# Another hand-written order for the first slots of a sparse-attention and FFN kernel

## The chip, the core and the metric

One Trainium2 chip, one of its cores. A core has a matrix engine (TensorE; PE in the profile, its weight loads PEld), a vector engine (VectorE, DVE), a scalar engine (ScalarE, ACT), GpSimd (POOL) and a queue engine for transfers (SyncE, SP), each with its own stream of instructions in a fixed order, and DMA engines that serve all queues. The metric is the device time of one execution in microseconds (us); lower is better. A time is the median of three runs; the profile is of one further execution.

## The reference

Attention with two sparse masks over 8 batches x 8 heads, 576 tokens, 64 wide, and then, for all 4608 tokens of width 512, a feed-forward network that multiplies two projections and has no nonlinear function:

```python
scores = scale * np.matmul(q, k.transpose(0, 1, 3, 2))
rel = pos[:, None] - pos[None, :]
mask_local = (rel >= 0) & (rel < 32)
mask_strided = (rel >= 0) & (pos[None, :] % 32 == pos[:, None] % 32)
masks = [mask_local if h < H // 2 else mask_strided for h in range(H)]
attn = softmax(np.where(masks, scores, -1e9)) @ v
x = attn.transpose(0, 2, 1, 3).reshape(4608, 512)
out = ((x @ w1) * (x @ w2)) @ w3 @ w_out        # w1, w2: 512x1024; w3: 1024x1024; w_out: 1024x512
```

## The kernel before, in words

**Pairs.** Two heads of a batch make a pair; there are 32, four to a batch. In each batch pairs 0 and 1 (of four) have the local mask, 2 and 3 the strided one. A pair i goes through these steps, each a small function of the code:

- `load_qk` (L88): q and k are loaded by GpSimd's queue with a cast to f16, into one of four tiles `s16` that q and k of a pair share. A local pair takes one DMA each for q and k (L100), a strided one two each, one a head (L105).
- `load_v` (L108): v of a local pair comes by SP's queue in f32 into `vsL`, three DMAs (L117, L119); `gate` puts a small memset on DVE ahead of it (L115). v of a strided pair comes by GpSimd's queue, four DMAs (L130).
- `emit_T` (L292): PE transposes q and k (L301) into two banks of the pool `psA`; copies bring them back, q's of a local pair on ACT or, where `cp` is given, on DVE (L309), q's of a strided pair on DVE (L314), k's on ACT (L309, L315).
- `emit_S` (L318): PE makes the scores in two banks of the pool `psF` (L333, L339), DVE adds the mask (L345).
- `emit_max` (L348), `emit_sub` (L356) on DVE, `emit_exp` (L364) on ACT.
- `emit_norm` (L375): DVE sums and inverts (L380, L382), then a product on GpSimd or, with `dve`, on DVE (L383).
- `emit_cast_v` (L277) and `shift_v` (L284), for local pairs: v's cast to f16 on GpSimd, ACT or DVE (L281), and a second copy of it, shifted by 32 rows, by two DMAs of SP.
- `emit_P` (L389): PE transposes the probabilities into a `psA` bank (L401) and ACT or DVE copies them out (L404). From pair 9 on a DMA does this.
- `emit_V` (L407): probabilities times v on PE in two `psF` banks (L421, L438), copied into `xT` by ACT and DVE (L426, L442 to L446).

`psA` has two banks and `psF` six; everything that PE writes draws on them.

**Weights.** w3 and w_out are multiplied once, into `wfh`. `load_w3(c)` (L210) loads two of the eight row groups of w3, a quarter of it, `load_wo(c)` (L207) a half of w_out, and `load_w` (L203) a half of w1 or w2. `fold_t(mc)` (L218) transposes a row group with eight matmuls (L223) and copies it (`w3T`, L225) on DVE or ACT; `fold_m(mc, half)` (L228) multiplies it by half of w_out, four matmuls (L233), and after the second half casts the result (L236).

**Masks.** `make_maskL` (L144) makes the local mask with four instructions on GpSimd and copies on ACT. `make_sel` (L159) makes a small pattern on GpSimd; `make_maskS` (L165) copies it twice on DVE (L168), multiplies it on PE (`mps`, L170), turns it into the mask on DVE (L172) and finishes it on GpSimd (L176).

**FFN.** Tokens go in nine chunks of 512. A chunk has eight a-pieces (x times w1, L248, copied by ACT, L252), eight b-pieces (x times w2, L258, multiplied on DVE, L261) and four out-pieces (times `wfh`, L269, copied by ACT, L274, stored by SP). `feed(us, batches)` (L475) puts pieces into the order until a credit in us is used up: 0.87 for an a- or b-piece, 1.74 for an out-piece. The first four a- and b-pieces of a chunk use the first halves of w1 and w2, the others the second halves.

**The order.** `manual_schedule` (L503) takes the instructions of each engine in the order in which these functions are called. Up to L674 this order is a list written out by hand: pairs 0 to 8, the folding of the weights and the first chunk. From L675 on (`for n in range(9, NP + 2)`) a loop gives the order for pairs 9 to 31. So each engine's queue is fixed, and an instruction that waits holds up all that stands behind it on its engine; for GpSimd, which issues most loads, that includes the loads.

Of the kernel before, what the change touches and what calls it, by code (L numbers as in the profile page):

```python
# [27 lines left out]
def kernel(  # L28
# [130 lines left out]
    def make_sel():  # L159
        nc.gpsimd.memset(sel, 1.0)  # L160
        for sg in (1, -1):
            nc.gpsimd.affine_select(out=sel, in_=sel, compare_op=ALU.is_ge, fill=0.0, base=0,
                                    pattern=[[0, 22], [sg, 3]], channel_multiplier=-sg)
# [327 lines left out]
    def zero_S():  # L491
        for t in qTS + prS:
            nc.vector.memset(t, 0.0)

    def zero_L(i):
        nc.vector.memset(kTL[i][:, 0:QB], 0.0)
        nc.vector.memset(vsL[i][HALF:P, LC - 1], 0.0)
        nc.vector.memset(vhL[i][0:QB, 0, 0], 0.0)
        nc.vector.memset(prL[i][:, LB, :], 0.0)
# [1 line left out]
    dve = nc.vector  # L501
    cp, act, pool = nc.vector.tensor_copy, nc.scalar.copy, nc.gpsimd.tensor_copy
    with tc.manual_schedule():  # L503
        zero_S()
        load_v(1)
        load_qk(0, "k")
        make_maskL()
        load_qk(1, "k")
        make_identity(nc, id16)
        load_qk(0, "q")  # L510
        load_qk(1, "q")
        load_v(0, True)
        load_w3(2, 2)
        load_qk(2, "k")
        load_qk(2, "q")
        make_sel()
        load_wo(0)
        load_qk(3, "k")
        zero_L(1)
        zero_L(0)  # L520
        emit_T(0, cp)
        load_w3(0, 2)
        emit_S(0)
        emit_T(1)
        load_qk(3, "q")
        emit_max(0)
        emit_cast_v(1, cp)
        nc.vector.memset(wz, 0.0)
        load_wo(4)
        make_maskS()  # L530
        load_v(3)
        emit_sub(0)
        emit_exp(0)
        emit_norm(0)
        emit_S(1)
        emit_T(2)
        fold_t(3, act)
        fold_t(2, act)
        emit_cast_v(0, cp)
        emit_max(1)  # L540
        load_w3(4, 2)
        emit_sub(1)
        load_qk(4, "k")
        emit_exp(1)
        fold_m(3, 0)
        load_qk(4, "q")
        fold_m(2, 0)
        emit_S(2)
        emit_norm(1)
        shift_v(0)  # L550
        emit_T(3)
        load_w(w1r, w1h, 0)
        load_v(2)
        fold_t(0, cp)
        fold_t(1, act)
        emit_P(0)
        emit_S(3)
        emit_max(3)
        load_w(w2r, w2h, 0)
        load_qk(5, "q")  # L560
        emit_max(2)
        fold_m(1, 0)
        shift_v(1)
        fold_m(1, 1, cp)
        fold_m(2, 1)
        load_qk(5, "k")
        emit_sub(3)
        fold_m(3, 1, cp)
        emit_sub(2)
        emit_exp(3)  # L570
        emit_norm(3)
        emit_P(1)
        fold_m(0, 0)
        emit_exp(2)
        fold_m(0, 1)
        fold_t(4, cp)
        fold_t(5, cp)
        emit_V(0)
        load_qk(6, "q")
        load_qk(6, "k")  # L580
        emit_V(1)
        emit_norm(2, dve)
        emit_T(4)
        fold_m(5, 0)
        load_w3(6, 2)
        fold_m(5, 1)
        emit_P(3)
        emit_P(2, cp)
        fold_m(4, 0)
        emit_V(2)  # L590
        emit_V(3)
        emit_S(4)
        load_qk(7, "k")
        feed(3.04, 1)
        emit_max(4)
        load_qk(7, "q")
        emit_sub(4)
        emit_T(5, cp)
        feed(2.61, 1)
        load_w(w1r, w1h, 1)  # L600
        emit_S(5)
        emit_T(6)
        emit_max(5)
        load_w(w2r, w2h, 1)
        emit_exp(4)
        fold_m(4, 1, cp)
        fold_t(6, act)
        fold_t(7, act)
        emit_sub(5)
        load_v(4, True)  # L610
        load_qk(8, "k")
        emit_T(7)
        emit_S(6)
        emit_max(6)
        fold_m(6, 0)
        fold_m(7, 0)
        emit_sub(6)
        emit_exp(6)
        emit_norm(4)
        load_qk(8, "q")  # L620
        emit_exp(5)
        load_v(5, True)
        emit_S(7)
        feed(1.46, 1)
        fold_m(6, 1)
        load_qk(9, "q")
        emit_norm(6, dve)
        emit_max(7)
        load_qk(9, "k")
        load_qk(10, "q")  # L630
        emit_cast_v(5, act)
        emit_norm(5)
        feed(0.43, 1)
        fold_m(7, 1, cp)
        emit_P(4, cp)
        emit_cast_v(4, act)
        feed(1.03, 1)
        load_v(6)
        shift_v(5)
        shift_v(4)  # L640
        load_qk(10, "k")
        load_v(8)
        load_v(10)
        feed(2.77, 1)
        emit_T(8)
        load_v(7)
        load_v(9, True)
        emit_sub(7)
        feed(2.17, 1)
        emit_P(6)  # L650
        emit_S(8)
        emit_exp(7)
        emit_norm(7, dve)
        emit_P(5, cp)
        emit_max(8)
        feed(2.17, 1)
        emit_sub(8)
        emit_T(9, cp)
        emit_V(4, cp)
        load_qk(13, "q")  # L660
        emit_V(5, cp)
        emit_exp(8)
        load_qk(12, "q")
        load_qk(11, "k")
        emit_V(6)
        emit_P(7)
        emit_cast_v(8, act)
        shift_v(8)
        load_qk(11, "q")
        emit_cast_v(9, cp)  # L670
        emit_norm(8)
        load_qk(13, "k")
        load_qk(12, "k")
        feed(3.17, 1)  # L674
        for n in range(9, NP + 2):  # L675
            full = (n - 1) // 4
            first = full - 1 if n % 4 == 1 else full
            f = 5.2
            if n < NP:
                shift_v(n)  # L680
                emit_S(n)
            if n + 1 < NP:
                emit_T(n + 1)
            if n + 5 < NP:
                load_qk(n + 5)
            for i in (n + 3, n + 2):
                if i < NP and where(i)[2] == (i == n + 3):
                    load_v(i)
            for i in (n - 3, n - 2):
                if i + (3 if by_dma(i) and i % 4 < 3 else 2) == n:  # L690
                    emit_V(i)
            if n < NP:
                emit_max(n)
            feed(0.1 * f, first)
            if n < NP:
                emit_sub(n)
                emit_exp(n)
                emit_norm(n)
                if n + 1 < NP:
                    emit_cast_v(n + 1)  # L700
            feed(0.15 * f, first)
            if n <= NP and not by_dma(n - 1):
                emit_P(n - 1)
            feed(0.55 * f, full)
            if n < NP and n % 2 == 1:
                for i in (n - 1, n):
                    if by_dma(i):
                        emit_P(i)
            feed(0.2 * f, full)
        feed(1e9, B)  # L710
# [31 lines left out]
```

## Time and profile before

| | us |
|---|---|
| median of three runs (lowest, highest) | 271.19 (270.99, 271.27) |
| the profiled execution | 270.49 |
| its span, first to last instruction | 268.7 |
| PE busy / DVE / POOL / ACT | 250.3 / 178.4 / 152.7 / 139.1 |
| PE's first transpose starts | 9.33 |
| PE's first fold_m starts | 18.00 |
| PE's first a-piece starts | 36.52 |
| PE reaches emit_S(9), the loop's first step | 67.68 |
| mean DMA rate over the span | 144 GB/s |

The profiled execution's own time is 1.8 us above its span. The page gives for each engine a busy share, then rows of 40 equal slices (6.7 us each) in tenths, then the chain of work that ended last, the costliest groups of instructions and the transfers. A "wait" names the engine and line that stood idle and what released it.

### The profile page before, as it was taken

To read this page: it belongs to the slowest core of one execution; us is meant where nothing else is said; L and a number is where in the kernel's file an instruction comes from. 1 tells how busy PE (TensorE), PEld (TensorE's weight loads), DVE (VectorE), ACT (ScalarE), POOL (GpSimd) and SP (SyncE) were. 2 spreads that over 40 slices of the span, in tenths; PEclk is the share of its full clock that TensorE was granted. 3 is DMA by queue.
4 is the path that set the end of the run, shared out by engine and by line. 5 is a ranking of instruction groups with operands and counts; after the bars stand their busy time and mean duration, and the time that the engine had idled before them with its cause. 6 is when DMAs were issued, how large, how long until landed. Compare 5 with 4: busy or idle time off the path is not lost.

```text
span 268.7 us, 9825 instructions
## 1 busy us (share of the span) xinstructions
PE 250.3 (93%) x4186; PEld 130.3 (48%) x4186; DVE 178.4 (66%) x357; ACT 139.1 (52%) x253; POOL 152.7 (57%) x236
## 2 busy tenths in 40 slices
PE   0288999999999999999999999999999999999995
PEld 0255656455554555554555455544554444444443
DVE  3378849999778768868886787678768823432210
ACT  3254756576655664666566466546655444333322
POOL 7688673498984896489468856886683110000000
PEclk9999999999999999999999999999999999999999
DMA  6999999999999699998998998996575152002113
GB/s 123 175 209 222 194 189 164 174 162 227 190 195 169 111 225 199 113 188 185 125 155 219 194 146 77 253 177 107 82 181 102 29 111 78 2 1 78 39 60 139
DMA packets 66237, 38.75 MB, mean 144 GB/s; under 512 B 45588, under 2 KB 60944, under 8 KB 66192
## 3 DMA queue, kind: packets, MB, share of 16 engines
q0 software_dynamic: 22112, 17.29, 43.3%
q1 hardware_dynamic: 44080, 20.82, 38.5%
q8 instruction: 33, 0.54, 0.8%
q14 instruction: 12, 0.10, 0.1%
HBM read 39.24 MB, written 9.44 MB: 181 GB/s over the span
## 4 chain that ended last, share of the span: by engine, by line
PE 75%; DMA 9%; DVE 8%; POOL 3%; issue 2%; ACT 2%; POOLq 0%; DVEq 0%; ACTq 0%
PE ops L269 22%; PE aps L248 20%; PE bps L258 20%; PE fps L233 3%; DMA w3s<-in_moe_w_dram 3%; DMA s<-in_q_dram 3%; PE tpq L301 2%; DMA s<-in_k_dram 2%; PE op L421 2%; PE sp L333 2%; DVE tmp L360 2%; PE op L438 1%; DMA vhS<-in_v_dram 1%; DVE tmp L345 1%; DVE sm L380 1%
## 5 line engine op out<-in xcount | busy, mean ns | idle before, releaser
L248 PE MATMUL aps<-xT,w1h 128*128 128x512 f16 x288 | 74.1, 380 | 0.1
L258 PE MATMUL bps<-xT,w2h 128*128 128x512 f16 x288 | 73.9, 379 | 0.0
L261 DVE TENSOR_TENSOR abt<-bps,asb 128x512 f16<-128x512 f32 x72 | 47.8, 679 | 32.1 <-PE bps L258 30.1
L269 PE MATMUL ops<-wfh,abt 128*128 128x512 f16 (+1 forms) x296 | 65.6, 374 | 0.2 <-DVE xT L426 0.2
L252 ACT COPY asb<-aps 128x512 f32<-128x512 f32 x72 | 41.4, 585 | 33.3 <-PE aps L248 20.0
L130 POOL DMA_DIRECT2D vhS<-in_v_dram x70 | 43.1, 755 | 3.1 <-DMA s<-in_k_dram 1.4
L258 PEld LDWEIGHTS <-w2h 128*128 128x128 f16 x288 | 28.1, 98 | 33.5
L269 PEld LDWEIGHTS <-abt 128*128 128x128 f16 x296 | 27.8, 98 | 30.7 <-issue 0.3
L248 PEld LDWEIGHTS <-w1h 128*128 128x128 f16 x288 | 27.0, 98 | 30.8
L274 ACT COPY osb<-ops 128x512 f32<-128x512 f32 (+1 forms) x36 | 20.7, 579 | 31.6 <-PE ops L269 28.8
L383 POOL TENSOR_TENSOR prS<-prS,rc 128x594 f16<-128x594 f16 x13 | 15.4, 1183 | 29.9 <-ACT asb L252 14.4
L383 POOL TENSOR_TENSOR prL<-prL,rc 128x576 f16<-128x576 f16 x16 | 19.2, 1200 | 13.6 <-DVE vsL L115 8.4
L360 DVE TENSOR_TENSOR tmp<-tmp,mx 128x576 f32<-128x576 f32 (+1 forms) x32 | 26.1, 816 | 0.9
L301 PE MATMUL tpq<-id,s 54*64 54x54 f16 (+1 forms) x640 | 17.4, 196 | 9.6 <-DMA s<-in_q_dram 9.6
L353 DVE TENSOR_REDUCE mx<-tmp 128x9 f32<-128x576 f32 (+1 forms) x32 | 24.2, 758 | 0.5
L105 POOL DMA_DIRECT2D s<-in_q_dram x35 | 21.2, 630 | 4.9 <-PE tpk L301 2.3
L105 POOL DMA_DIRECT2D s<-in_k_dram x35 | 21.9, 686 | 2.8 <-DMA s<-in_q_dram 2.0
L372 ACT ACTIVATE prS<-tmp 128x594 f16<-128x594 f32 x16 | 11.2, 700 | 20.8 <-DVE tmp L360 14.0
L301 PEld LDWEIGHTS <-s 54*64 54x64 f16 (+1 forms) x1280 | 14.4, 112 | 12.1 <-DMA s<-in_q_dram 9.7
L380 DVE TENSOR_REDUCE sm<-prS 128x11 f32<-128x594 f16 x16 | 12.3, 770 | 9.9 <-ACT prS L372 9.9
L345 DVE TENSOR_TENSOR tmp<-sp,maskL 128x320 f32<-128x320 f32 (+1 forms) x32 | 13.1, 450 | 8.4 <-PE sp L333 8.3
L380 DVE TENSOR_REDUCE sm<-prL 128x9 f32<-128x576 f16 x16 | 12.0, 753 | 9.8 <-ACT prL L372 9.8
(78 smaller groups left out, 272.9 us busy)
## 6 DMA issues: line engine op xcount, KB each, us to landing
out_dram<-osb SPq DMA_DIRECT2D x35, 256.0 KB, 3.2
vsL<-in_v_dram SPq DMA_DIRECT2D x32, 128.0 KB, 5.2
s<-in_k_dram POOLq DMA_DIRECT2D x16, 144.0 KB, 5.0
s<-in_q_dram POOLq DMA_DIRECT2D x16, 144.0 KB, 4.2
s<-in_k_dram POOLq DMA_DIRECT2D x31, 74.2 KB, 5.1
s<-in_q_dram POOLq DMA_DIRECT2D x31, 74.2 KB, 5.4
w3s<-in_moe_w_dram POOLq DMA_DIRECT2D x4, 512.0 KB, 7.4
vhL<-vhL SPq DMA_DIRECT2D x16, 120.0 KB, 3.8
```

What stands on the lines that cost most here:

```text
L105: nc.gpsimd.dma_start(t[p0 + r0[0]:p0 + r0[1], h, 0:n * D], _ap(src[b, h0 + h], 0 + ap[0], ap[1] + [[1, n * D]]))
L130: nc.gpsimd.dma_start(vt[HALF * half + r0[0]:HALF * half + r0[1], h, 0:m * D], _ap(v[b, h0 + h], 6 * half * D + ap[0], ap[1] + [[1, m * D]]))
L248: nc.tensor.matmul(aps, cols(w1h, ci, jc), xT[ci][:, c * NT:(c + 1) * NT], start=(ci == 0), stop=(ci == KC1 - 1))
L252: nc.scalar.copy(out=asb, in_=aps)
L258: nc.tensor.matmul(bps, cols(w2h, ci, jc), xT[ci][:, c * NT:(c + 1) * NT], start=(ci == 0), stop=(ci == KC1 - 1))
L261: nc.vector.tensor_mul(abts[c][:, jc, :], bps, abts.pop((c, jc)))
L269: nc.tensor.matmul(ps, abts[c][:, jc, ts * P:(ts + 1) * P], wfh[:, jc, n * w:n * w + w], start=(jc == 0), stop=(jc == KC2 - 1))
L301: nc.tensor.transpose(tp[HALF * h:HALF * h + HALF, s, :], s16[p0:p0 + npar, h, s * D:(s + 1) * D], id16[p0:p0 + npar, p0:p0 + npar])
L353: nc.vector.tensor_reduce(out=mx, in_=tmp, axis=AX.X, op=ALU.max)
L360: nc.vector.tensor_tensor(out=tmp, in0=tmp, in1=_sub(mx, 0, P, 0, [[1, nt], [0, w]]), op=ALU.subtract)
L380: nc.vector.tensor_reduce(out=sm, in_=prv, axis=AX.X, op=ALU.add)
L383: eng.tensor_tensor(out=prv, in0=prv, in1=_sub(rc, 0, P, 0, [[1, nt], [0, w]]), op=ALU.mult)
```

## The change

The list between `manual_schedule` and the loop is replaced by another order of the same calls; no function and no line of the loop is touched. All pairs, folds and pieces appear in both. What differs:

- **loads**: v of pairs 1 and 0 still come first on SP, now with k of pair 0 between them in the text and q of pair 1 behind; v of pair 0 loses its `gate`. GpSimd's queue was k0, maskL, k1, identity, q0, q1, w3(2), k2, q2, sel, w_out(0), k3, w3(0), q3, w_out(4), maskS, v3, norm(0), w3(4). It becomes k0, q1, maskL, sel, q0, k2, k1, identity, w3(2), q2, w_out(0), w3(0), maskS, k3, q3, w_out(4), w3(4), v3, cast_v(0).
- **mask**: `make_maskS` stands between S(0) and T(1), ahead of max(0); it stood behind max(0), a cast of v and a memset of `wz`.
- **PE's order** to the first a-piece: it was T0 S0 T1 mps S1 T2, fold_t 3, 2, fold_m (3,0) (2,0), S2 T3, fold_t 0, 1, P0 S3, fold_m (1,0) (1,1) (2,1) (3,1), P1, fold_m (0,0) (0,1), fold_t 4, 5, V0 V1 T4, fold_m (5,0) (5,1), P3 P2, fold_m (4,0), V2 V3 S4. It becomes T0 S0 mps T1, fold_t 2, S1 T2, fold_t 3, S2, fold_m (2,0) (3,0), fold_t 0, 1, T3, fold_m (0,0) (1,0) (1,1), S3 P0, fold_m (2,1), P1, fold_t 5, fold_m (3,1) (0,1), P2, fold_m (5,0), V0, fold_t 4, T4 V1, fold_m (5,1), P3 V2, fold_m (4,0), V3 S4.
- **engines**: from DVE to ACT go the copies of fold_t 0, 4, 5, cast_v(1), and pT of pairs 2 and 5, q of T(9), and half of V(4)'s and V(5)'s; from ACT to DVE go q of T(1), pT of pairs 1, 3, 6 and 7, the copy of fold_t 6 and cast_v(5). norm(0)'s product goes from GpSimd to DVE, cast_v(0) from DVE and cast_v(8) from ACT to GpSimd.
- **behind the first a-piece**: the credits were 3.04, 2.61, 1.46, 0.43, 1.03, 2.77, 2.17, 2.17, 3.17 and become 3.04, 2.61, 1.46, 2.17, 2.77, 1.03, 2.17, 2.30, 1.30, the same sum; V(4) and V(5) come before the last two credits; k of pair 12 is loaded early and v of pair 10 late.

The diff up to the first piece of the FFN:

```diff
@@ -501,177 +501,177 @@
     dve = nc.vector
     cp, act, pool = nc.vector.tensor_copy, nc.scalar.copy, nc.gpsimd.tensor_copy
     with tc.manual_schedule():
-        zero_S()
         load_v(1)
         load_qk(0, "k")
+        load_v(0)
+        zero_L(1)
+        load_qk(1, "q")
+        zero_L(0)
         make_maskL()
+        make_sel()
+        load_qk(0, "q")
+        load_qk(2, "k")
         load_qk(1, "k")
         make_identity(nc, id16)
-        load_qk(0, "q")
-        load_qk(1, "q")
-        load_v(0, True)
         load_w3(2, 2)
-        load_qk(2, "k")
+        zero_S()
+        emit_T(0, cp)
         load_qk(2, "q")
-        make_sel()
         load_wo(0)
-        load_qk(3, "k")
-        zero_L(1)
-        zero_L(0)
-        emit_T(0, cp)
         load_w3(0, 2)
         emit_S(0)
-        emit_T(1)
+        make_maskS()
+        emit_T(1, cp)
+        load_qk(3, "k")
         load_qk(3, "q")
+        load_wo(4)
         emit_max(0)
-        emit_cast_v(1, cp)
-        nc.vector.memset(wz, 0.0)
-        load_wo(4)
-        make_maskS()
+        fold_t(2, act)
+        emit_S(1)
+        emit_T(2)
+        load_w3(4, 2)
+        fold_t(3, act)
         load_v(3)
         emit_sub(0)
+        emit_max(1)
         emit_exp(0)
-        emit_norm(0)
-        emit_S(1)
-        emit_T(2)
-        fold_t(3, act)
-        fold_t(2, act)
-        emit_cast_v(0, cp)
-        emit_max(1)
-        load_w3(4, 2)
+        emit_cast_v(1, act)
         emit_sub(1)
+        emit_S(2)
+        emit_max(2)
+        emit_cast_v(0)
+        fold_m(2, 0)
+        emit_exp(1)
         load_qk(4, "k")
-        emit_exp(1)
+        emit_norm(0, dve)
+        load_qk(4, "q")
         fold_m(3, 0)
-        load_qk(4, "q")
-        fold_m(2, 0)
-        emit_S(2)
+        fold_t(0, act)
+        fold_t(1, act)
+        emit_sub(2)
+        load_w(w1r, w1h, 0)
         emit_norm(1)
+        shift_v(1)
+        emit_exp(2)
+        emit_T(3)
+        fold_m(0, 0)
+        fold_m(1, 0)
+        fold_m(1, 1, cp)
+        nc.vector.memset(wz, 0.0)
+        emit_S(3)
+        emit_P(0)
+        emit_norm(2, dve)
+        emit_max(3)
+        fold_m(2, 1)
+        load_v(2)
+        emit_P(1, cp)
+        emit_sub(3)
+        fold_t(5, act)
+        fold_m(3, 1, cp)
+        fold_m(0, 1)
+        emit_P(2)
+        emit_exp(3)
         shift_v(0)
-        emit_T(3)
-        load_w(w1r, w1h, 0)
-        load_v(2)
-        fold_t(0, cp)
-        fold_t(1, act)
-        emit_P(0)
-        emit_S(3)
-        emit_max(3)
         load_w(w2r, w2h, 0)
         load_qk(5, "q")
-        emit_max(2)
-        fold_m(1, 0)
-        shift_v(1)
-        fold_m(1, 1, cp)
-        fold_m(2, 1)
+        fold_m(5, 0)
         load_qk(5, "k")
-        emit_sub(3)
-        fold_m(3, 1, cp)
-        emit_sub(2)
-        emit_exp(3)
         emit_norm(3)
-        emit_P(1)
-        fold_m(0, 0)
-        emit_exp(2)
-        fold_m(0, 1)
-        fold_t(4, cp)
-        fold_t(5, cp)
         emit_V(0)
+        fold_t(4, act)
         load_qk(6, "q")
+        emit_T(4)
+        emit_V(1)
+        fold_m(5, 1)
+        emit_P(3, cp)
+        emit_V(2)
+        load_w3(6, 2)
+        fold_m(4, 0)
+        emit_V(3)
         load_qk(6, "k")
-        emit_V(1)
-        emit_norm(2, dve)
-        emit_T(4)
-        fold_m(5, 0)
-        load_w3(6, 2)
-        fold_m(5, 1)
-        emit_P(3)
-        emit_P(2, cp)
-        fold_m(4, 0)
-        emit_V(2)
-        emit_V(3)
+        load_qk(7, "q")
         emit_S(4)
...
```

## The prediction

> **What bounds the kernel now.** I read the page first: TensorE's busy slices, then the chain that ended last, then the waits of PE and of POOL up to 40 us, then the timelines of PE, POOL, DVE and ACT up to 80 us, and last the landing time of each load in the trace.
>
> ```profile
> PE 250.3 (93%) x4186; PEld 130.3 (48%) x4186; DVE 178.4 (66%) x357; ACT 139.1 (52%) x253; POOL 152.7 (57%) x236
> PE   0288999999999999999999999999999999999995
> DMA  6999999999999699998998998996575152002113
> ```
> TensorE is busy for 250.3 of 268.7 us. Of the 18.4 us that it stands still, 9.3 lie before its first instruction and some 3.3 behind its last. The DMA row is full from the second slice to about slice 23: early on, an order of loads can only say what lands first.
>
> ```profile
> PE tpq L301 <- DMA s<-in_q_dram: 9.6, 2, 9.3
> PE mps L170 <- DVE sel L168: 1.9, 1, 1.9
> PE sp L333 <- DVE qT L309: 0.9, 1, 0.9
> PE fps L233 <- ACT w3T L225: 0.8, 2, 0.5
> ```
> These are all PE waits of size in the first 36 us: the first q, then mask's matmul (1.94), then small ones. Only these can be won in the front.
>
> ```profile
> core 0: us, PE busy (x) PEld busy (x) DVE busy (x) ACT busy (x) POOL busy (x), PEclk, DMA share, GB/s
> 9.33:18.00 8.67, 5.62 (x205) 4.70 (x206) 5.95 (x16) 4.22 (x7) 5.54 (x12) 1.00 1.08 198
> 18.00:36.52 18.52, 17.41 (x374) 10.60 (x375) 14.84 (x30) 11.36 (x20) 15.39 (x22) 1.00 1.15 205
> 36.52:67.68 31.16, 30.93 (x563) 16.34 (x552) 27.66 (x55) 18.93 (x32) 19.73 (x31) 1.00 1.03 181
> ```
> I cut at PE's own marks: 9.33 first transpose, 18.00 first fold_m, 36.52 first a-piece of the FFN, 67.68 emit_S(9), where the loop begins. The loop is unchanged, and so is each stretch's set of PE work up to S(9). So the whole question is when PE reaches 36.52 and 67.68. Behind 18.00 hardly 1.5 us of idle are left in those two stretches, so the ceiling of a gain is low.
>
> **Rows for the loads.** The chain and POOL's timeline show the queue:
>
> ```profile
> 5.66 7.45 DMA w3s<-in_moe_w_dram
> ...
> 13.39 0.58 POOL L212 DMA_DIRECT2D w3s<-in_moe_w_dram  x1 [2.01 <-DMA w3s<-in_moe_w_dram]
> ...
> 24.39 0.82 POOL L205 DMA_DIRECT2D w1h<-in_moe_w_dram  x1 [0.24 <-DMA woh<-in_moe_w_out_dram]
> ```
> POOL's 13th load is issued at 13.39, 0.28 after its 5th landed; the 18th at 17.83, after the 10th landed (17.55); the 24th at 24.39, after the 16th (24.10); the 29th at 29.06, after the 21st (28.78). So in this kernel a POOL load waits for the landing of the one eight before it, and whatever stands behind it on POOL waits too. From the packets, the 16 engines work about 1.0 us on a local q or k, 0.85 on a strided one, 2.7 on a 512 KB piece of w3 or w_out, 0.95 on a strided v; landings follow 1 to 1.8 us behind.
>
> **Part 1: up to the first fold_t.** POOL now issues k0, q1, makes maskL (1.22 us, 2.11 to 3.33 before), sel (1.16, 8.45 to 9.61 before), and only then q0, at about 5.1 instead of 4.50; then k2 and k1 (0.62 an issue) and the identity, done near 8.1 (before 4.55). The SP loads of v are issued as before (the old one waited for nothing at its memset: 2.60, then 2.64). With fewer bytes ahead of it, q0 lands near 9.0; T(0) at 9.0 (bounds 8.6 to 9.6), S(0) 1.55 later as now, its adds end 3.17 after T(0). The old order has max(0), a cast and wz's memset between those adds and sel's copies; gone, so mps goes at 12.4, not 14.11. But T(1) now stands behind mps: 12.55 to 13.25 (before 11.47). S(1) is no longer next: fold_t(2) is, and it needs w3's second quarter. That quarter has k2's 0.85 us more ahead of it: landing 13.11 + 0.85 + about 0.2 = 14.2. S(0)'s matmuls end at 11.15, so the old wait of 1.94 at mps turns into 1.2 ahead of mps and 0.95 ahead of fold_t(2); whether T(0) goes at 8.6 or 9.6 changes the one against the other and not fold_t(2). Then, at the rows' slow early times, fold_t 0.87, S(1) 0.60, T(2) 0.96, fold_t(3) 0.87, S(2) 0.60: fold_m(2,0) at 18.15. w_out's first half has the same bytes ahead as before, 17.55 + 0.2, so it isn't later. The old order stands at fold_m at 18.00 with S(2) still to do (0.67 with its wait): **a lead of 0.5 us**.
>
> **Part 2: 18.15 to the first a-piece.** The old stretch is 18.52 long; take off S(2) with its wait 0.67, the wait for w3T 0.53, the hold inside S(4) 0.46 and 0.2 of scraps: 16.7 of work, the same in both. What waits does the new order add?
> - fold_m(1,1) needs w_out's second half, landing 24.1 + 0.2; PE is there at 23.9: 0.4. The old order did four halves of work before it and didn't need it earlier.
> - fold_t(5) comes ahead of fold_m(3,1) and (0,1). Its w3 quarter landed at 28.78; it gives up v's 0.95 ahead of it and about 0.45 of shift_v's traffic: 27.6. PE is there at 26.95: 0.65 (0 to 1.2).
> - P(3). These copies decide it:
>
> ```profile
> 23.12 1.01 ACT L225 COPY w3T<-w3tp 128x1024 f16<-128x1024 f16 x1 [0.42 <-PE w3tp L223]
> ...
> 32.44 0.68 ACT L309 COPY qT<-tpq 128x576 f16<-128x576 f16 x1
> 32.97 0.69 ACT L309 COPY kTL<-tpk 128x576 f16<-128x576 f16 x1
> ```
> ```profile
> 30.36 1.29 DVE L225 COPY w3T<-w3tp 128x1024 f16<-128x1024 f16 x2
> ```
> fold_t(0), (4) and (5) leave DVE (0.64 each) for ACT (0.97 each), cast_v(1) too (0.48 to 0.72); DVE gets T(1)'s qT (0.75), norm(0)'s product (0.78) and pT of pairs 1 and 3. In sum ACT has 2.3 us more in the front, DVE 0.9 less. Behind P(2)'s copy (to 31.2) ACT has exp(3), which waits for sub(3) on DVE, 31.9; V(0)'s two copies 32.55; w3T(4) 33.5; then qT and kT of T(4), 34.1 and 34.7. P(3) needs one of T(4)'s two psA banks; norm(3) on POOL comes out at the same 34.1, since POOL stood behind v2's loads, which wait for that w3 quarter. PE is there at 33.4: 0.75 (0 to 1.2).
> - S(4) needs two of the six psF banks that V(2) and V(3) hold until ACT has copied: 0.4 (0.46 now).
>
> Sum: 18.15 + 16.7 + 0.4 + 0.65 + 0.75 + 0.4 = **37.05**, against 36.52: the lead is spent, 0.5 behind (bounds: 35.3 with none but the w_out wait, 38.05 with all at their upper ends).
>
> POOL's product norm(1) stays behind w1's load, which waits for w_out's second half (24.3): done at 26.5, before P(1) at 26.65, so nothing. cast_v(0) on POOL costs 0.71 by the loop's rows, with SP's shift and 3.8 us of landing, ready by 28.5 for V(0) at 31.0: nothing; without that cover 1.2.
>
> **Part 3: 37.05 to S(9).** DVE does 27.66 of 31.16 us here, so its queue is what to replay. It gains ft6's copy 0.68, a cast 0.48, one pT, and loses T(9)'s 0.75 and V(4), V(5) 0.75. In my replay PE meets no late w1 or w2 half (before: landed 47.7 for a piece at 49.7); b-products come out up to 2 us late on DVE, and the last one at 61.0 is needed by the first out-piece's last matmul at 61.7; V(5)'s copies hold a bank for 0.5; against that the old order's stretch has 0.4 at P(7) and 0.2 of idle. Length 31.0 to 31.3, against 31.16. I take 31.25.
>
> **The number.** +0.53 + 0.09 = +0.6 us. The profiled run took 270.49 with its span at 268.7; the median of the three is 271.19, 0.7 above it. The difference is put on the median: 271.8; a profiled span would read about 269.3.
>
> **A rule weighed.** The first eight matmuls of fold_m take 2.65 us, the same eight later 1.89: 0.76 for a slow start, though the granted clock reads 1.00 in every stretch; their starts are 427 ns apart four times, then 216. I keep that 0.76 in both orders. [...]
>
> **Rivals.**
> 1. *The lead survives* (faster). Place: ACT's copies from 28 to 34 us. If w3's quarter lands by 26.95 and T(4)'s copies are out by 33.4, the waits 0.65 and 0.75 go, and PE is at its first a-piece near 35.7. The next piece needs w2's half, which landed at 36.47 and has the same bytes ahead: b0 could go at 36.7 instead of 37.39. That caps the lead at 0.7: 270.5. For it: ACT is only 61% busy in that stretch now. Against: three long copies are put just there. It decides from a sum of waits under 0.9.
> 2. *DVE late in part 3* (slower still). Three b-products wait at once behind norm(6) and adds of S(7); each holds a psF bank of six. If a further copy is in line, V(4) or the out-pieces wait some 0.75 each, twice: +1.5, 273.3. For it: 9 tenths busy DVE. Against: ACT lighter, T(9) off DVE.
> [...]
>
> Chances: forecast (271.3 to 272.4) 0.45, of which 0.2 below 271.7; rival 1 (270.2 to 270.8) 0.30, nearly all of it below 270.65; rival 2 0.20; rival 3 0.05. What a measurement of this kernel can tell from no change is about 0.2%, 0.54 us. So faster 0.29, within 0.21 (0.2 of the forecast, 0.01 of rival 1), slower 0.50 (0.25 + 0.20 + 0.05). The range takes rival 1 in its greater part and rival 2's lower: 270.3 to 273.2.
>
> **What would show it.** Right: mps' wait near 1.2, a PE wait near 0.95 for w3 before L223, one for w3T or w3s near 27, P(3) behind L309 on ACT, first aps near 37.0, S(9) near 68.3. Wrong: w3's second quarter landing before 13.3; first aps before 36.2; or a wait over 1 us in 45 to 66, which this replay doesn't have.

## The result, and the profile after

The new order takes 274.27 us (median of 17 runs, 271.66 to 276.21) against 271.27 (17 runs) for the old one on the same chip: ratio 1.0107 [1.0077, 1.0137]. It is slower, as forecast, but by 3.0 us and not by 0.6, and outside the range. The profiled execution took 274.05 (before 270.49), its span 272.3 (268.7).

The page after, busy time of the engines and the slices of PE and of its granted clock:

```profile
PE 252.8 (93%) x4186; PEld 130.8 (48%) x4186; DVE 178.8 (66%) x353; ACT 139.5 (51%) x254; POOL 153.0 (56%) x237
PE   0379999997999999999999999999999999999995
PEclk9999999999799999999999999999999999999999
```

The work is the same; PE has 2.5 us more busy time, and slices 10 and 11 (from 61 to 75 us) show where: in the one PE stands still for a part, in the other its clock is granted at less. All marks in us below are of one profiled execution of each kernel. PE's waits up to 110 us:

```profile
PE tpq L301 <- DMA s<-in_q_dram: 8.2, 1, 8.2
PE w3tp L223 <- DMA w3s<-in_moe_w_dram: 3.1, 2, 2.9
PE op L421 <- ACT osb L274: 1.7, 1, 1.7
PE mps L170 <- DVE sel L168: 1.2, 1, 1.2
```

The second line is a wait of 2.9 in the front where 0.95 was forecast; the third, V(5) behind a copy of the first out-piece, was not in the forecast's replay. Two of the same cuts as before, and two slices at that wait:

```profile
core 0: us, PE busy (x) PEld busy (x) DVE busy (x) ACT busy (x) POOL busy (x), PEclk, DMA share, GB/s
36.52:67.68 31.16, 29.07 (x594) 15.62 (x594) 27.13 (x51) 15.70 (x28) 20.63 (x34) 1.00 1.04 174
9.33:18.00 8.67, 4.25 (x164) 3.58 (x165) 3.97 (x11) 2.07 (x4) 5.50 (x11) 1.00 0.97 165
66.00:68.00 2.00, 1.12 (x36) 0.63 (x36) 1.93 (x4) 1.94 (x5) 2.00 (x5) 0.85 1.05 158
68.00:70.00 2.00, 2.00 (x6) 0.76 (x5) 1.93 (x3) 1.83 (x5) 2.00 (x5) 0.50 1.05 221
```

From 9.33 to 18.00 the DMA engines moved 165 GB/s (before 198). From 68 to 70 PE is fully busy at half clock. PE's own marks, in us:

| PE reaches | before | forecast | after | after minus before |
|---|---|---|---|---|
| first transpose | 9.33 | 9.0 | 8.19 | -1.14 |
| first fold_m | 18.00 | 18.15 | 19.44 | +1.44 |
| first a-piece | 36.52 | 37.05 | 38.37 | +1.85 |
| emit_S(9) | 67.68 | 68.3 | 73.15 | +5.47 |
| first a-piece of the second chunk | 71.27 | | 76.22 | +4.95 |
| end of the last out-piece | 265.36 | | 269.01 | +3.65 |

So there are two losses: about 1.3 beyond the forecast before the first fold_m, and 3.6 between the first a-piece and S(9). Some 1.8 comes back behind that, 0.5 of it before the second chunk. The old order has small stalls of its own there: PE waits 0.36 at V(7) and 0.39 at V(8).

Such marks vary between executions. Five traces of the new front (this one, e1, e3, e5, e9) have the first a-piece at 37.23 to 38.82, three of the old front (before, e10, e18) at 36.52 to 36.82. So the front is later in all five, but a step of under 1 us between two kernels with the new front is not told from chance.

### The profile page after: what moved, and what is told of

The parts are those of the page before. It is cut to its first block, busy times and chain, and to the rows that moved or that the text cites. A ratio compares the mean times of both kernels' runs of the same rounds, so it can differ in the third digit from the quotient of the medians.

```text
span 272.3 us, 9823 instructions
## 1 busy us (share of the span) xinstructions
PE 252.8 (93%) x4186; PEld 130.8 (48%) x4186; DVE 178.8 (66%) x353; ACT 139.5 (51%) x254; POOL 153.0 (56%) x237
## 4 chain that ended last, share of the span: by engine, by line
PE 83%; DMA 7%; POOL 3%; DVE 2%; ACT 2%; issue 2%; POOLq 0%; DVEq 0%; ACTq 0%
PE ops L269 23%; PE aps L248 22%; PE bps L258 22%; PE fps L233 5%; DMA woh<-in_moe_w_out_dram 4%; DMA w3s<-in_moe_w_dram 3%; PE tpq L301 3%; PE op L421 2%; PE sp L333 2%; PE sp L339 2%; PE op L438 1%; POOL s L105 1%; PE tpk L301 1%; PE w3tp L223 1%; POOL s L100 1%
## 5 line engine op out<-in xcount | busy, mean ns | idle before, releaser
L269 PE MATMUL ops<-wfh,abt 128*128 128x512 f16 (+1 forms) x296 | 67.5, 381 | 0.1
L274 ACT COPY osb<-ops 128x512 f32<-128x512 f32 (+1 forms) x36 | 20.7, 576 | 31.1 <-PE ops L269 24.5
L383 POOL TENSOR_TENSOR prL<-prL,rc 128x576 f16<-128x576 f16 x15 | 18.9, 1257 | 12.9 <-PE aps L248 6.3
L360 DVE TENSOR_TENSOR tmp<-tmp,mx 128x576 f32<-128x576 f32 (+1 forms) x32 | 25.3, 790 | 0.9
```

What stands on the lines that cost most here:

```text
L269: nc.tensor.matmul(ps, abts[c][:, jc, ts * P:(ts + 1) * P], wfh[:, jc, n * w:n * w + w], start=(jc == 0), stop=(jc == KC2 - 1))
L360: nc.vector.tensor_tensor(out=tmp, in0=tmp, in1=_sub(mx, 0, P, 0, [[1, nt], [0, w]]), op=ALU.subtract)
L383: eng.tensor_tensor(out=prv, in0=prv, in1=_sub(rc, 0, P, 0, [[1, nt], [0, w]]), op=ALU.mult)
```

## Where the second loss comes from: three theories

The trace shows a chain backwards from V(5). On ACT the copy of the out-piece (L274) stands behind exp(7), which waits for sub(7) on DVE:

```profile
65.65 0.70 ACT L372 ACTIVATE prS<-tmp 128x594 f16<-128x594 f32 x1 [2.72 <-DVE tmp L360]
66.26 0.57 ACT L274 COPY osb<-ops 128x512 f32<-128x512 f32 x1
```
```profile
66.88 0.46 PE L421 MATMUL op<-pT,vhL 64*64 64x32 f16 x34 [1.65 <-ACT osb L274]
67.27 3.51 PE L269 MATMUL ops<-wfh,abt 128*128 128x512 f16 x8
```

Two things are to be seen: ACT idles 2.72 for DVE while a copy that frees a bank stands ready in its queue, and the eight matmuls of the out-piece behind V(5) take 3.51 (their starts span 3.30; 1.74 at full rate). **First theory:** only the order on ACT is wrong. **Second:** pair 7's whole chain comes too late in the list. **Third:** DVE itself is late, because some of its instructions take far longer than their rows in the old profile. For the third, DVE and POOL at two places:

```profile
53.03 1.49 DVE L360 TENSOR_TENSOR tmp<-tmp,mx 128x594 f32<-128x594 f32 x1
...
59.09 1.97 DVE L383 TENSOR_TENSOR prS<-prS,rc 128x594 f16<-128x594 f16 x1
...
68.85 1.78 DVE L383 TENSOR_TENSOR prS<-prS,rc 128x594 f16<-128x594 f16 x1
```
```profile
52.74 1.15 POOL L383 TENSOR_TENSOR prL<-prL,rc 128x576 f16<-128x576 f16 x1 [6.35 <-PE aps L248]
...
59.07 1.35 POOL L383 TENSOR_TENSOR prL<-prL,rc 128x576 f16<-128x576 f16 x1
...
68.98 1.00 POOL L281 CAST vhL<-vsL 128x640 f16<-128x640 f32 x1
```

The columns are start, length, engine, line. A sub or product of DVE takes 0.78 elsewhere. These three take 1.49, 1.97 and 1.78, and each lies over a product or a cast of GpSimd (1.15, 1.35 and 1.00 long). Together that is 1.92 too long before 63 us and 1.0 behind it. In the old order no sub or product of DVE is stretched by more than 0.1 up to the second chunk; norm(6)'s product there:

```profile
52.90 0.78 DVE L383 TENSOR_TENSOR prS<-prS,rc 128x594 f16<-128x594 f16 x1
```

## The experiments

Every ratio is against the kernel before on the same chip. "Chunk 2" is the first a-piece of the second chunk.

**e1, the copy ahead of exp(7)** (first theory against "the wait only moves").

```diff
         emit_sub(7)
-        emit_exp(7)
         load_qk(11, "q")
         feed(2.17, 1)
+        emit_exp(7)
```


> The changed kernel with emit_exp(7) put behind the out-piece that follows it, nothing else. Theory 1 (ACT's copy of the first out-piece stands behind exp(7), which waits for sub(7) on a late DVE; V(5) then waits 1.65 us for that bank, and the clock at half for 3.41 us behind it costs 1.7): V(5)'s wait goes, the granted clock shows no half-rate stretch at 67, the first a-piece of the second chunk moves from 76.2 to about 73, the span falls by 2 to 3.3 us, time near 271.5. Rival (DVE's queue itself is late, and the wait only moves to another instruction in 62 to 70): the span falls by under 0.6 us, time near 274.

1.0088 [1.0052, 1.0124]. V(5) no longer waits, but P(7) now waits 1.2 for norm(7) on DVE and T(10) 0.6; chunk 2 at 75.87. The first theory falls: ACT's order only chose who waits for DVE.

**e2, k of pair 2 behind w3's second quarter** (the front).

```diff
         load_qk(0, "q")
-        load_qk(2, "k")
         load_qk(1, "k")
...
         load_w3(2, 2)
+        load_qk(2, "k")
```


> The changed kernel with the two strided loads of k of pair 2 put behind the load of w3's second quarter. Theory (those two loads hold up the quarter by more than their mean share of the DMA engines): the quarter lands at or before 13.7 instead of 15.22, fold_t(2) starts at about 13.7, w_out's half stays near 19.4 or comes a little earlier, the first a-piece comes 0.3 to 0.8 earlier than 38.37; time 273.5 to 274. Rival (q0 issued late leaves the engines half empty from 7 to 12 us, whatever the order): the quarter lands at 14.5 or later, and the first a-piece stays within 0.3 of 38.37; time unchanged at 274.3.

1.0075 [1.0041, 1.0108]. The quarter landed at 12.98 (15.22), w_out's half at 17.84 (19.39), but the first fold_m moved only to 18.28 (19.44) and the first a-piece to 37.41 (38.37), which is inside the spread of this front. A new wait of 0.8, labelled "issue", stands inside S(2); more on it at e16.

**e3 and e4, each half of the change alone.** e3 has the new order up to emit_S(4) and the old one behind it; e4 the old order up to there (with q of pair 7 loaded) and the new one behind it.

```diff
     with tc.manual_schedule():
-        zero_S()
         load_v(1)
...
         emit_V(3)
         emit_S(4)
```
```diff
         emit_V(3)
+        load_qk(7, "q")
         emit_S(4)
-        load_qk(7, "k")
         feed(3.04, 1)
...
```


> The changed order up to emit_S(4), then the order of before (q of pair 7 is loaded where the order of before loads it). If the front alone costs, the first a-piece stays near 38.4 (36.52 before) and the end is 1 to 1.9 us later than before: 272.3 to 273.1. If the front's loss is hidden later, 271.3 to 271.8.

> The order of before up to emit_S(4) (with q of pair 7 loaded ahead of it), then the changed order. Theory 1: the first a-piece stays near 36.5, the wait of V(5) and the half-rate stretch behind it appear as in the changed kernel, time 272.5 to 273.5. Rival (the wait comes only of a late front, since DVE falls behind there): no wait of over 0.6 us at V(5), time within 0.5 of before.

e3: 1.0025 [0.9986, 1.0064], first a-piece 38.82, chunk 2 at 73.50, no wait at V(5). e4: 1.0054 [1.0019, 1.0089], first a-piece 37.18, chunk 2 at 73.34, V(5) waits 1.6. So the rest costs about 0.54%, 1.5 us, alone. The front's 0.25%, 0.7 us, is not clear of no change. What the two leave of the 1.07% is within the intervals.

**e5, pair 7's chain earlier** (second theory).

```diff
         emit_exp(6)
+        emit_S(7)
...
+        emit_max(7)
         emit_norm(6, dve)
+        emit_sub(7)
+        emit_exp(7)
```


> The changed kernel with the scores of pair 7 taken ahead of cast_v(5), its maximum ahead of norm(6) and its subtraction and exponential behind that, some 8 us earlier on every engine; the work is the same. Theory 2 (the new order starts pair 7's chain on DVE too late, when PE has only three out-pieces left to cover it, so moving one copy only moves the wait): no PE wait of over 0.6 us from 60 to 77, no half-rate stretch there, the second chunk's first a-piece near 73 instead of 76.2, time 271.3 to 272.5. Rival (DVE has too much work in all in this stretch, so it is late whatever the order): waits of 1 us or more stay somewhere from 60 to 77, time over 273.2.

1.0100 [1.0047, 1.0154], chunk 2 at 75.86; now P(6) waits 2.2 behind a copy on ACT (L309). The second theory falls.

**e6, e2's front with the old rest.**

```diff
         load_w3(2, 2)
         load_qk(2, "k")
+        zero_S()
+        emit_T(0, cp)
...
```


> The changed order up to emit_S(4) with k of pair 2 behind w3's second quarter, then the order of before. If the pieces add up: the front of the changed order with the order of before behind it had 271.9, and moving k of pair 2 gave 1.0 of 274.3 at the same place, so 270.9, at or just below before; first a-piece near 37.5. Rival (what the front wins is hidden in the rest): 271.7 to 272.1.

1.0011 [0.9976, 1.0046]: not to be told from e3 or from no change. S(2) has a wait "issue" of 1.6, and V(7) one of 1.5 for v.

**e7, k of pair 1 behind the quarter instead.**

```diff
-        load_qk(1, "k")
         make_identity(nc, id16)
         load_w3(2, 2)
+        load_qk(1, "k")
```


> The changed kernel with k of pair 1, one local load of 128 packets of 1152 B, put behind w3's second quarter, where the run before had put k of pair 2, two strided loads of 108 packets of 1408 B in all. If bytes ahead are what counts, the quarter lands at 14.1 or earlier, as much sooner as with pair 2. If strided loads hold up what is behind them more than their bytes do, it lands at 14.3 to 14.8 only. T(1) waits for its k here, so the time says nothing.

One run, 275.89; T(1) waits for its k, so the time tells little. The quarter was issued at 7.41, 0.59 earlier, and landed at 14.38, 0.84 earlier. By the expectation's bounds that is its second case, strided loads; but the earlier issue, which the expectation left out, accounts for 0.59 of the 0.84. In e2 the issue was 1.25 earlier (6.75) and the landing 2.24.

**e8, the old order with 24 matmuls of zeros in idle places of PE** (is the slow start on the path?).

```diff
+        nc.vector.memset(wz, 0.0)
+        warm(16)
         zero_S()
...
```


> The kernel of before with 24 matmuls of zeros, added work whose result nobody reads, where PE stands still: 16 ahead of T(0), 2 behind it, 4 behind T(1), 2 behind fold_t(2); the memset of their zeros goes first. Theory (the matmuls before some 20 us run at half rate because the array has seen no dense work until fold_m; dense work of any kind releases it): the full rate begins before 14, fold_m(3,0) takes 0.86 instead of 1.62, the first a-piece comes 0.8 to 1.5 earlier than 36.52, time 269.8 to 270.7. Rival (the release hangs on something else, or comes no sooner since transposes let it fall back): full rate still begins at 19 to 23, and the added matmuls cost 0.4 to 1.7: time 271.5 to 273.

1.0029 [0.9992, 1.0066]. Full rate came at 4.99 (before 19.55), was lost from 15.23 to 18.64, and the first a-piece came at 36.53, as without them (36.52). So the earlier full rate won nothing here: fold_m began 0.55 later (18.55), behind the added work, and what its faster matmuls saved ended in a longer wait for q of pair 3. T(3) starts at 21.29, before at 21.25.

**e9, products apart** (third theory): the new order with three edits that only stop DVE and GpSimd from meeting.

```diff
+        emit_sub(6)
         emit_norm(4)
...
-        emit_sub(6)
...
-        emit_norm(5)
         emit_norm(6, dve)
+        emit_norm(5)
...
-        emit_cast_v(8)
+        emit_cast_v(8, act)
```


> The changed kernel with sub(6) ahead of norm(4), norm(6) ahead of norm(5), and cast_v(8) on ACT instead of GpSimd, so that GpSimd's products no longer run beside DVE's sub(6), and norm(6)'s and norm(7)'s products on DVE. Theory 3 (a DVE instruction that reads two tiles in SBUF stands while GpSimd runs an instruction that reads SBUF: 0.73, 1.19 and 1.00 us over the usual 0.77 in the changed kernel, nothing in the same stretch of before; that is DVE's lateness): sub(6) takes 0.77 and both products 0.78, V(5)'s wait is 0.6 or less, the second chunk's first a-piece comes at 72.5 to 74.5 instead of 76.2, time 271.3 to 272.8. Rival (DVE is late from the copies that moved to it): the durations fall, but V(5) or P(7) still waits 1 us or more; time 273.5 or more.

1.0031 [1.0004, 1.0059]. The product of norm(6), which took 1.97:

```profile
57.28 0.78 DVE L383 TENSOR_TENSOR prS<-prS,rc 128x594 f16<-128x594 f16 x1
```

V(5) waits 0.5 instead of 1.7, no half clock follows, and from the first a-piece (38.03) to chunk 2 (73.06) it takes 35.03; the new order needs 37.85, the old one 34.75. The third theory holds for the chain: without the meetings DVE is in time, and the wait and the half clock go. In time that is 0.76% of the 1.07%, give or take 0.4 by the two intervals. e11 and e14 take the same edits to other fronts.

**e10, the reverse: the old order with norm(5) just ahead of norm(6)**, and **e18**, the same again.

```diff
+        emit_norm(5)
         emit_norm(6, dve)
...
-        emit_norm(5)
```


> The kernel of before with norm(5) moved next to norm(6), ahead of it, so that GpSimd's product of norm(5) falls on DVE's product of norm(6); nothing else. Theory 3: norm(6)'s product takes 1.5 to 2.0 instead of 0.78, and DVE's queue behind it comes out up to 1.2 later; a PE wait of up to 1 us appears between 52 and 66; time 0 to 1 us over before: 271.3 to 272.6. Rival (those long durations came of something else in the changed order): norm(6)'s product stays at 0.78.

> The kernel of e10_before_products_together (the old order with emit_norm(5) moved just ahead of emit_norm(6, dve)) once more, on another chip, with more runs. e10 was 0.6% faster than the kernel before; with the mask first as well (e15) nothing was left of that. If the gain is the order's own, the ratio is 0.991 to 0.997 again. If e10's runs were a lucky draw, as the unchanged marks of its profile say (first a-piece 36.82 against 36.52, chunk 1's 71.81 against 71.27), the ratio is 0.998 to 1.003.

e10: 0.9940 [0.9911, 0.9969]; e18: 0.9957 [0.9921, 0.9992]. My expectation missed. GpSimd's product began 0.76 ahead, DVE's took 1.06, so only 0.28 was lost: how the two fall in time counts, not that they stand side by side in the list. And this order is faster than the old one, by about half a per cent. Why is open: in e10's profile chunk 2 comes at 71.81, 0.5 later than in the old one. In the loop, at 77.53, the old order has a meeting of its own, a sub of 1.97; it takes 1.14 in e10 and is not stretched in e18. But in e12, which has no gain, it is not stretched either.

**e11, e9 and e2 together.**

```diff
         load_w3(2, 2)
+        load_qk(2, "k")
...
-        emit_cast_v(8)
+        emit_cast_v(8, act)
```


> The run with the products apart, and besides k of pair 2 behind w3's second quarter. If both causes are real and add up, as they did one at a time: 270.7 to 271.8, at or near before. If the front's 0.5 to 1 us is hidden in the rest: the same as with the products apart alone.

1.0023 [0.9995, 1.0050]. The first a-piece comes at 37.03, 1.0 earlier than in e9, but the time is the same: a wait of 1.1, again "issue", stands in chunk 2's first a-piece. Against e2, which has the same front, e9's edits are worth 0.52%.

**e12, the old order with the mask's matmul early**, and **e15**, that with e10's edit.

```diff
         emit_T(1)
+        make_maskS()
...
-        make_maskS()
         load_v(3)
```


> The kernel of before with one part of the change alone: make_maskS right behind T(1), so that mask's copies on DVE come ahead of max(0) and of the cast of v. Theory (the front is held by the landing of loads, not by mask): mps goes at about 12.8 instead of 14.11, S(1) at 13.4 or so instead of 14.26, but fold_m still starts at 17.6 to 18.0 with w_out's half; the first a-piece moves by 0 to 0.4; time 270.9 to 271.5. Rival (mask's wait of 1.94 is on the path): the first a-piece comes 0.7 or more earlier, time 270.6 or less.

> The kernel of before with norm(5) ahead of norm(6), which had 270.0, and make_maskS right behind T(1), which had changed nothing. If the first was a gain of its own (P(5)'s and the later steps' waits end sooner): 269.8 to 270.4, below before. If it was chance of those runs: 271.0 to 271.5.

e12: 0.9984 [0.9954, 1.0015]. PE's wait at mps fell from 1.94 to 0.55, yet fold_m came at 18.13, behind a wait of 1.0 for w_out's half: PE's largest wait behind the first q was not on the path. e15: 1.0026 [0.9997, 1.0054], without e10's gain.

**e13, GpSimd's mask work behind the quarter's issue**, and **e14**, that with e9's edits.

```diff
         zero_L(0)
-        make_maskL()
-        make_sel()
         load_qk(0, "q")
...
         load_w3(2, 2)
+        make_maskL()
+        make_sel()
```


> The changed kernel with make_maskL and make_sel behind the issue of w3's second quarter, so that GpSimd issues q0, k2, k1 and that quarter 2.3 us earlier (at 5.7 instead of 8.0, as in before) in the same order of bytes. If the quarter was late because it was issued late: it lands at 13.2 or earlier (15.2 in the changed kernel, 13.1 in before with 0.85 us of bytes less ahead). If it was late because of the bytes of k2 ahead of it alone, as the prediction had it: 13.9 to 15.2. In either case w_out's half lands at 17.5 to 18.0 instead of 18.8, the first a-piece comes 0.5 to 1 earlier, and the time falls by 0.3 to 1 to about 273.5, since what lies behind 50 us is unchanged.

> The same and GpSimd's products apart from DVE's. If the late loads and the products together are all that the change costs: no difference to before, 270.8 to 271.7. If something else of the changed order costs time, 272 or more, as with the products apart alone (272.3).

e13: 1.0065 [1.0041, 1.0090]. With the same bytes ahead of it, but issued at 5.70 instead of 8.00, the quarter landed at 13.27 instead of 15.22. So it was late because it was issued late. Yet fold_m came at 18.78. e14: 1.0039 [1.0007, 1.0071], fold_m at 18.52. With this front e9's edits take V(5)'s wait from 1.7 to 0.6 and the half clock away as well, and chunk 2 comes at 72.89 instead of 75.22. But they are worth only 0.26%, which is not clear of noise: the third chunk begins at the same time in both (100.4). Between lie, in e14, a wait "issue" of 1.41 at 74.69 and a sub of DVE stretched to 1.76. So what the meetings cost at the end is shown only roughly, 0.26 to 0.76% in three pairs of runs; and with both causes away 0.39% is left, by e14's expectation a sign that something else costs time too. S(2) in e14:

```profile
16.49 0.47 PE L339 MATMUL sp<-kT,qTS 64*64 64x54 f16 x18
18.33 0.26 PE L339 MATMUL sp<-kT,qTS 64*64 64x54 f16 x4 [1.38 <-issue]
```

The first 18 of its 22 matmuls run, then PE stands for 1.38 in the middle of S(2), and no engine or transfer is named as what it waits for.

**e16 and e17, e14 with 64 or 128 tiny matmuls (64x64, of zeros) ahead of everything.** In the traces so far all but one of these gaps (e8's of 0.65, near the 1728th) stand at PE's 450th and 2498th instruction (matmuls and weight loads counted), 8 x 256 apart. They end 1.29 to 1.50 us after the end of a 16384 byte packet of the instruction queue. The page of the old order counts these packets (queue, kind: packets, MB, share of 16 engines):

```profile
q8 instruction: 33, 0.54, 0.8%
```

PE's matmuls and weight loads there are 4186 each, 8372 for 33 packets, 254 to one. So, as an estimate, a packet holds 256 of PE's instructions, an eighth of the distance above, and 64 matmuls with their weight loads are half of one.

```diff
     with tc.manual_schedule():
+        nc.vector.memset(wz, 0.0)
+        warm(64)
         load_v(1)
...
```


> The kernel of e14_masks_behind_and_apart with 64 small matmuls of zeros (64x64, each with its weight load) put on TensorE ahead of everything, where it only waits for the first q. Nothing of the rest changes, but every later TensorE instruction has a number higher by 128. Theory: the waits labelled issue are for TensorE's own program. In seven traces the gap stands at its 450th instruction (in S(2)) or its 2498th (in an a-piece), 8 x 256 apart, and ends 1.29 to 1.50 us after the end of a 16384 byte packet of the instruction queue; 16384 bytes are 256 instructions of 64. Then 128 more ahead move the border out of S(2): no gap of over 0.5 us there, S(2) begins behind fold_t(3) without the 1.4, the first fold_m near 17.2 instead of 18.52, and the gap at the a-piece near 73 goes as well or moves by 128 instructions. Time: if the later waits don't take it back, 0.5 to 1.3 below e14, near 271.4. Rival, that the gap comes from what S(2) needs (a bank, a copy, k of pair 2) under a wrong label: it stays at S(2), 1.2 to 1.6 long, fold_m at 18.3 to 18.7, and the time is that of e14, 272.3.

> As e16_half_block_of_instructions, with 128 small matmuls of zeros instead of 64, so that every later number is higher by 256, a whole packet of instructions. Theory of the instruction packets: the border falls on the same place of S(2) again, and so the gap of 1.0 to 1.6 is back there and ends 1.3 to 1.5 after the end of a packet of the instruction queue; fold_m at 18.2 to 18.8; time as e14, 272.3, give or take 0.5. Rival one, that dummy matmuls ahead help by themselves (the clock, or a warm queue): no gap, as with 64. Rival two, a wrong label: a gap with 0, with 64 and with 128.

S(2) with 64, and then with 128 (`warm(128)`):

```profile
16.74 0.52 PE L339 MATMUL sp<-kT,qTS 64*64 64x54 f16 x22
17.19 0.56 PE L233 MATMUL fps<-woh,w3T 128*128 128x512 f16 x1
```
```profile
16.78 0.47 PE L339 MATMUL sp<-kT,qTS 64*64 64x54 f16 x18
18.38 0.26 PE L339 MATMUL sp<-kT,qTS 64*64 64x54 f16 x4 [1.14 <-issue]
18.58 0.61 PE L233 MATMUL fps<-woh,w3T 128*128 128x512 f16 x1
```

With half a packet of instructions more, the gap is gone and fold_m comes at 17.19; with a whole packet it is back at the same place, behind the same 18 matmuls, and ends 1.35 after its packet. So the wait goes with the place in PE's own program. In e16 the border then fell on another small-matmul stretch, where PE stood 2.75 at 46.9: e16 took 274.31 in four runs that scatter too much for a ratio, e17 1.0031 [0.9991, 1.0072]. The shift moves the wait; the 0.5 to 1.3 us that was expected of e16 did not show.

## Why the prediction was off, step by step

Two steps failed, a landing in the front and the replay of DVE's queue behind it. The second carries most of the error.

**Up to the first fold_m.** Right: mps goes 3.4 behind T(0) after a wait of 1.2, as forecast; T(0), and with it mps at 11.57, came 0.8 earlier than forecast, and that didn't matter, as said. **The first step that failed is the landing of w3's second quarter, "13.11 + 0.85 + about 0.2 = 14.2".** It landed at 15.22 (in four more runs of this front 14.84 to 15.84), and w_out's half at 19.39 instead of 17.75. I counted the bytes ahead of it, but not the issue, 2.3 later than before. The prediction itself had GpSimd done at 8.1 "(before 4.55)" and didn't use it:

```profile
8.00 0.58 POOL L212 DMA_DIRECT2D w3s<-in_moe_w_dram  x1
```

Issue to landing was 7.45 before, 7.2 after, 6.97 in e7, 7.57 in e13. The bytes ahead count too: with k of pair 2 out of the way it was 6.23 in e2 and 6.6 in e11. The DMA engines moved less in between, 165 against 198 GB/s from 9.33 to 18.00, and e13, in which GpSimd issues all from q0 to the quarter 2.3 earlier in the same order, shows that the issue decides. The wait at fold_t(2) was therefore 2.9 and not 0.95. But an earlier landing would not have given all of that back: S(2)'s 450th instruction started 1.50 after its packet here too, at 18.95, at the same bound as the gaps of e2, e6, e13 and e14. In the old order the 450th came at 20.67, 4.7 behind its packet.

**The full rate came later as well in this execution**, to which the prediction gave 0.05. The trace's first record of the granted clock, at full, begins at 23.03 instead of 19.55. Both halves fold_m(2,0) and (3,0) took 1.7, where before the second took 0.9; their matmuls start 426 or 427 ns apart up to 22.40, in the old order 216 from 19.62 on. (The first starts of the old order are 399, 427, 427 and 370 ns apart, not 427 four times; the sum stays.) Inside one trace the recorded changes of rate lie apart by multiples of 3.413 us: 23.03 and 67.40 by 13 of them, 67.40 and 70.81 by one, in e8 4.99 and 15.23 by three. Matmuls of zeros brought the full rate forward (4.99 in e8); otherwise no run shows what sets it. It differs between executions: full rate came at 20.42 to 23.03 in five traces of this front and at 19.50 to 20.74 in three of the old one, so the delay is only in part the order's.

**From there to the first a-piece.** 18.93 against a forecast of 18.9, but by errors that offset, so this is luck. Of the waits listed there, 2.2 in sum, PE shows only P(3)'s, 0.38 and not 0.75. At fold_t(5) it shows none: the quarter landed at 28.72, later than the 27.6 forecast, but PE came there only at 29.16. The late full rate took 0.85; some 1.0 more is spread over the stretch and not placed.

**From the first a-piece to S(9): 34.8 against 31.25. This is the second step that failed, and most of the error.** The replay took each DVE instruction at its length in the old profile. It said that a wait over 1 us between 45 and 66 would prove it wrong, and V(5)'s 1.65 begins at 65.2. Rival 2 named the symptom, DVE late and V waiting for a bank, and gave it 0.20 and 273.3; its cause, a further copy in line, was not the one. The runs showed another cause: 1.92 us of stretched DVE instructions before 63 put DVE late. On PE that cost V(5)'s 1.65, and then the clock: from 63.99 to 67.40 PE was busy for 1.76 of 3.41, nearly all of it small matmuls and transposes, and from 67.40 to 70.81 it ran at half rate (granted 0.50), 3.30 for an out-piece of 1.74, which is another 1.6. The two are 3.25 of the 3.5 in this execution. Not every one has the second: 9 of the 17 runs have a mean granted clock of 0.994 or less, as one such stretch gives (half of 3.41 is 0.6% of 272), and lie about 274.5 in the median; the others lie at 273.5. So about 1 us hangs on the clock, and the new order is slower without it too.

In the trace a stretched instruction of DVE ends only behind GpSimd's: the three here end 0.63 to 0.64 after it, the product at 59.09 1.19 too long beside an instruction of 1.35. That is so also at 68.85, where DVE's recorded start lies 0.13 ahead of GpSimd's. The replay set DVE's subs and products beside GpSimd's at their old 0.78. The old profile has such a meeting itself, a sub of 1.97 at 77.53; that row was the missing check.

**The sum.** The prediction gave 0.53 us to the front and 0.09 to the rest. Alone, the front (e3) is not told from no change, and the rest (e4) costs 1.5 us, for a reason that the replay didn't have. So the sign came out right mostly by luck.

## What to carry to other kernels

In a hand-made order, replay the issue time of each load and not only the bytes ahead of it (issued 2.3 earlier, w3's quarter landed 1.95 earlier in e13), and look for instructions of DVE and GpSimd that will now run at the same time: an instruction's length in the old profile holds only beside the old neighbours (here 0.78, and up to 1.97 beside a product of GpSimd). A wait that leads a list of waits can lie beside another that ends later (e12), so look at what the same engine needs next before paying for its removal. Take away the suspected meeting alone (e9) before reordering whole chains (e1, e5).

## What the runs showed of the hardware

- The waits of PE with the label "issue", those of 0.6 to 2.75 us, stand in these traces in or just behind stretches of many small matmuls, all before 75 us, where the DMA row is still full. They stand only at PE instructions whose numbers are multiples of 256 apart (to within 2), and end 1.29 to 1.50 after a 16384 byte packet of the instruction queue. The 33 packets for 8372 instructions of PE, and the wait's place in e16 (gone from S(2)) and e17 (back, 1.14), agree with a wait for PE's own program.
- In the new order half rate came back behind 3.41 us (63.99 to 67.40) in which PE stood still for 1.65 and was busy for 1.76, nearly all of it small work. In e4 the same wait, 1.56 from 63.96 to 65.52, lies across 64.67, which is 20.30, where e4's full rate began, plus 13 of 3.413, and no half rate followed; in the new order it lies between two such marks, 63.99 and 67.40. That its place between the marks decides is an estimate from these two cases. The old order can show half rate too. Of e18's 12 executions three had a mean granted clock of 0.994 or less, at 272.4 to 273.8; the median of the others was 270.2. With the new order it was 9 of 17. The profiled one of e18's three has a wait "issue" of 1.61 that ends at 67.47, and half rate from 67.29 to 70.70.
- In the 20 traces every sub or product of DVE of 1.0 us or more, 41 of them, lies over an instruction of GpSimd (in the old and the new order a product or a cast) and ends 0.61 to 0.65 after that one's end, also where DVE's recorded start is the earlier, as here in the old order (77.53 + 1.97 is 0.65 behind 77.65 + 1.20):

```profile
77.53 1.97 DVE L360 TENSOR_TENSOR tmp<-tmp,mx 128x594 f32<-128x594 f32 x1
```
```profile
77.65 1.20 POOL L383 TENSOR_TENSOR prL<-prL,rc 128x576 f16<-128x576 f16 x1
```

So what DVE lost in these cases is what is left of GpSimd's instruction, less about 0.13: 1.19 to a product that began 0.02 ahead, but only 0.28 to one that began 0.76 ahead and had 0.41 left (e10).
